# Attention and two FFN layers on one core: value products in a bank per tile, first queries loaded from ScalarE's queue, the second score pair moved behind the layer's first block, and a spare PSUM bank for one more block

## Chip, cores and metric

The kernel runs on one core of one Trainium2 chip. The metric is device time in microseconds of one execution; every time before the change is from three timed runs and one profiled execution.

## What is computed

```
scores = (q @ k.T) / 8; causal mask; a = softmax(scores); local = a @ v      # B=2, H=8, S=576, D=64
q_p = phi(q); mem = (q_p @ M_prev) / (q_p . z_prev + 1e-6)                   # phi = elu + 1
x = sigmoid(beta) * mem + (1 - sigmoid(beta)) * local                        # laid out as 1152 tokens x 512
x = relu(x @ w_in)^2 @ w_out                                                 # first layer, 512 -> 2048 -> 512, weights wider than fp32
out = sum_e p[:, e] * (relu(x @ w1[e]) @ w2[e])                              # four experts, 512 -> 1024 -> 512
```

## The kernel before

The 1152 tokens are nine tiles of 128, in three chunks: chunk 0 is tiles 7 and 8 (the first 128 positions of both batches), chunk 1 is tiles 0 to 3, chunk 2 is tiles 4 to 6. Attention of a chunk runs beside the first layer of the chunk before it, so the program has an **opening** (attention of chunk 0, and the first scores of chunk 1), a **first stage** (layer of chunk 0, with the rest of chunk 1's attention, about 20 to 133 us), a **second stage** (layer of chunk 1 with chunk 2's attention), then the layer of chunk 2 and the experts.

Attention works on pairs: the same heads of two tiles. `s_` makes the score matmuls of a pair into two PSUM buffers (tag `s`, of which the first stage has two), the row maxima by VectorE (`top`, L189), then the exponentials by ScalarE (L319). `t_` transposes on TensorE (`atp`), and a copy brings it to SBUF (`at`); `v_` multiplies by the values (`pv`). `phis` makes phi(q), `mem` multiplies it by the memory (`pm`).

In the opening a string of steps sets the order on every engine. Chunk 0's four units are (tile 7, heads 0-3), (8, 0-3), (7, 4-7), (8, 4-7). Before, a bank `pv` held four heads of both tiles, and `local(0)` (step `x0`) read both banks before `v1` and `v3` wrote tile 8's half of them. `c0.load(0)` issues the first keys and queries, and `beta` (tile `bt`) is loaded ahead of it on ScalarE's queue; the gate made from `bt` (L172, then L174 to L176 on VectorE) stands ahead of the first row maxima on VectorE.

The first layer works in 16 blocks f of 128 hidden columns: `up(f)` (four matmuls for chunk 0, `hpa`), squared ReLU (`g`), and two blocks later `down(f-2)` (four matmuls, `y`). Its weights come as 64-bit words (`w`, 512 KB a half block), which ScalarE (`mag`, `bits`, L694 and L697) and VectorE (L700, L703) turn into fp32; the result is used and also written to DRAM (`w1s`), from where chunk 1's and chunk 2's layers read it back (`wraw`).

`mix(main, side, ratio, due)` puts `ratio` steps of attention behind each step of the layer. On TensorE the program's order holds; on the other engines outside the opening a list scheduler decides, and SyncE issues nearly all DMAs in the order that it gives. DMAs take eight semaphores in turn (DMAHW0 to DMAHW7), so each issue waits until the eighth DMA before it has landed. In `up`, a block's sums go to the bank `h`, of which there is one, or for a block named `spare` to a buffer of the tag `s`.

Of the kernel before, what the change touches and what calls it, by code (L numbers as in the profile page):

```python
# [21 lines left out]
P = 128  # L22
B, H, S, D = 2, 8, 576, 64
# [14 lines left out]
CHUNKS = [(7, 9), (0, 4), (4, 7)]  # L38
# [14 lines left out]
def attention_then_experts(ctx, tc, qa, ka, va, qc, kc, vc, mz, beta, w1, probs, w2, out):  # L53
# [11 lines left out]
    nc = tc.nc  # L65
# [99 lines left out]
    bt = kv.tile([P, H], F32, name="bt")  # L165
# [61 lines left out]
    ka_t, va_t = {}, {}  # L227
# [29 lines left out]
    def attention_a(c, pool, eng, banks):  # L257
# [9 lines left out]
        def load(r):  # L267
            raw = pool.tile([P, H, P], F32, tag="qa", name="qa", bufs=2)
            ka_t[r] = kva.tile([P, H, P], F32, name=f"ka{r}")
            for hs in (slice(0, 4), slice(4, 8)):  # L270
                nc.sync.dma_start(out=ka_t[r][:, hs], in_=ka[r, :, hs])
                nc.sync.dma_start(out=raw[:, hs], in_=qa[r, :, hs])
            q[r] = [raw, None, pool.tile([P, B, H, D + 1], F32, tag="xm", name="xm", bufs=2)]
            if r:
                load_v(r)
# [63 lines left out]
        def v_(u):  # L339
            t, kn, h0, nh = u  # L340
            b = TILES[t][0][0]
            at = at_.pop(u)
            half = t - b, h0 // 4
            if b == 0 and h0 % 4 == 0:
                pvs[half] = banks[0].tile([P, B, H // 2, D], F32, tag="pv", name="pv", bufs=banks[3])
            pv = pvs[half]
            for i in range(nh):
                for k in range(kn // P):
                    j = i * kn + k * P
                    for p in range(0, P, 64):  # L350
                        nc.tensor.matmul(
                            pv[p:p + 64, b, h0 % 4 + i, :], lhsT=at[:, j + p:j + p + 64], rhs=va_t[b, k][:, h0 + i, :],
                            start=(k == 0), stop=(k == kn // P - 1),
                        )
            if c and b and (h0 + nh) % 4 == 0:
                if half[1] == 0:
                    xls[t - b] = pool.tile([P, B, H, D], F32, tag="xl", name="xl", bufs=2)
                nc.scalar.activation(out=xls[t - b][:, :, h0 + nh - 4:h0 + nh], in_=pv, func=AF.Copy)
# [46 lines left out]

        def local(b):
            xl = xls[b] = pool.tile([P, H, D], F32, tag="xl0", name="xl0", bufs=2)
            for i in range(2):
                hs = slice(4 * i, 4 * i + 4)
                nc.vector.tensor_mul(xl[:, hs], pvs[CHUNKS[0][0], i][:, b], fs[0][:, b, hs, None].to_broadcast([P, 4, D]))  # L410
            nc.vector.tensor_add(xl, xl, q[0][2][:, b, :, 0:D])

        def out_(b):
# [296 lines left out]
    def ffn1(c, ps, gp, nh, cv=None):  # L710
        t0, t1 = CHUNKS[c]
        n = (t1 - t0) * P
        per = 512 // n
        gs, ws = {}, {}

        todo = [x for g in range(n1 + 1) for x in ((g, 0), (g - 2, 1)) if 0 <= x[0] < n1] + [(n1 - 1, 1)]
        raws = {}

        def fetch(ahead):
            while c and todo and len(raws) < ahead:  # L720
                x = todo.pop(0)
                raws[x] = wrp.tile([P, DM], F32, tag="wraw", name="wraw")
                nc.sync.dma_start(out=raws[x], in_=w1s[x])

        def prep(f, half):
            if c == 0:
                while (f, half) not in made:
                    next(cv)
                ws[f, half] = made.pop((f, half))
                next(cv, None)  # L730
                return
            fetch(1)
            raw = raws.pop((f, half))
            w = wp.tile([P, 2, DM], F32R, tag=f"w{half}", name=f"w{half}")
            on_vector = ((f < 3, f % 4 == 3), (False, f % 2))[c - 1][half]
            split(w, raw, nc.vector if on_vector else nc.gpsimd)
            ws[f, half] = w
            fetch(2)

        def up(f):  # L740
            spare = c == 1 and f == 1
            hp = (ps if spare or f % nh else ps_h).tile([P, n], F32, tag="s" if spare else "h", bufs=2 if spare else 1, name="hp" + "abc"[c])
            yield from mm_in(c, hp, ws.pop((f, 0)))
            r = gp.tile([P, n], F32, tag="r", name="r") if c else gp.tile([P, n], F32, tag="g", name="g0", bufs=3)
            nc.scalar.activation(out=r, in_=hp, func=AF.Relu)
            nc.vector.scalar_tensor_tensor(out=r, in0=hp, scalar=0.0, in1=r, op0=ALU.max, op1=ALU.mult)  # L746
            if c == 0:
                gs[f] = r
                return
            g = gp.tile([P, 2, n], F32R, tag="g", name="g", bufs=3)  # L750
            nc.scalar.activation(out=g[:, 0], in_=r, func=AF.Copy)  # L751
            nc.vector.tensor_sub(g[:, 1], r, g[:, 0].bitcast(F32))  # L752
            gs[f] = g

        def down(f):
            w, g = ws.pop((f, 1)), gs.pop(f)
            for d in range(NK):
                first, last = f == 0 and d % per == 0, f == n1 - 1 and d % per == per - 1
                if c == 0:
                    nc.tensor.matmul(yacc[d], lhsT=w[:, d * P:(d + 1) * P], rhs=g, start=first, stop=last)  # L760
                for i, (a, b) in enumerate(PASS if c else ()):
                    nc.tensor.matmul(  # L762
                        yacc[d], lhsT=w[:, a, d * P:(d + 1) * P], rhs=g[:, b],
                        start=(first and i == 0), stop=(last and i == 2),
                    )
                for k in range(d - per + 1, d + 1) if last else ():
                    nc.scalar.activation(out=y_of(c)[:, k], in_=yacc[k], func=AF.Copy)
                yield

        prep(0, 0)  # L770
        ps = (yield) or ps
        banks = [ps.tile([P, per, n], F32, tag=f"y{d}", name=f"y{d}") for d in range(NK // per)]
        yacc = [banks[d // per][:, d % per, :] for d in range(NK)]
        for f in range(n1 + 2):
            if f + 1 < n1:
                prep(f + 1, 0)
            if 1 <= f <= n1:
                prep(f - 1, 1)
            if f < n1:
                yield from up(f)  # L780
            if f >= 2:
                yield from down(f - 2)
        for k in range(NK):
            junk = gp.tile([P, n], F32, tag="r", name="junk")
            nc.scalar.activation(out=junk, in_=y_of(c)[:, k], func=AF.Square, accum_out=ysq[:, c, k:k + 1])

    with ExitStack() as ca:
        kva = ca.enter_context(tc.tile_pool(name="kva", bufs=1))
        aap = ca.enter_context(tc.tile_pool(name="aap", bufs=2))
        cvp = ca.enter_context(tc.tile_pool(name="cvp", bufs=2))  # L790
        cv = convert(cvp)
        mzd = kva.tile([P, H, B, D + 1], F32, name="mzd")
        with tc.tile_pool(name="ps_0", bufs=1, space=PSUM) as ps_0:
            with tc.manual_schedule():
                nc.scalar.dma_start(out=bt, in_=beta.partition_broadcast(P))

                wt = aap.tile([P, 512], BF16, name="wt")
                nc.vector.memset(wt, 0.0)
                warm = ps_h.tile([P, 512], F32, tag="h", name="warm")
                for _ in range(8):  # L800
                    nc.tensor.matmul(warm, lhsT=wt[:, 0:P], rhs=wt, start=True, stop=True)
                nc.gpsimd.memset(ones, 1.0)
                masks()
                layer = ffn1(0, None, gp, 2, cv)
                banks = [ps_0, 3, 2, 2]
                c0, c1 = attention_a(0, aap, nc.vector, banks), attention_a(1, aap, nc.gpsimd, banks)
                c0.load(0)
                for b in range(B):
                    bs = slice(D * b, D * b + D)
                    nc.gpsimd.memset(mzd[bs, :, 1 - b], 0.0)  # L810
                    nc.sync.dma_start(out=mzd[bs, :, b], in_=mz[bs, b])
                c0.load_v(0)
                opening(c0, c1, layer)
        nc.sync.dma_start(out=mzt, in_=mz[0:D])
        with tc.tile_pool(name="ps_1", bufs=1, space=PSUM) as ps_1:
            banks[:] = ps_1, 2, 1, 1
            layer.send(ps_1)
            mix(layer, rest(c1, value_scale(aap, banks)), 0.58)
    with ExitStack() as cb:
        bp = cb.enter_context(tc.tile_pool(name="bp", bufs=1))  # L820
        with tc.tile_pool(name="ps_2", bufs=1, space=PSUM) as ps_2:
# [346 lines left out]
```

## Time and profile before

| | |
|---|---|
| median of 3 runs | 727.13 us (726.19 to 728.55) |
| the profiled execution | 726.71 us, of which the span of its profile is 724.9 us |
| busy over the span | TensorE 679.4 us (94%), VectorE 548.1 us (76%), ScalarE 428.2 us (59%), GpSimd 239.3 us (33%) |
| chain that ended last | TensorE 51%, VectorE 19%, ScalarE 12%, DMA 7%, issue 6%, GpSimd 3% |

Busy time is the sum over an engine's instructions; the chain is followed back from the last instruction to whatever released it each time. TensorE is nearly full as a mean, but not in the opening and the first 40 us, where the DMA queues are.

### The profile page before, as it was taken

To read this page: it belongs to the slowest core of one execution; us is meant where nothing else is said; L and a number is where in the kernel's file an instruction comes from. 1 tells how busy PE (TensorE), PEld (TensorE's weight loads), DVE (VectorE), ACT (ScalarE), POOL (GpSimd) and SP (SyncE) were. 2 spreads that over 40 slices of the span, in tenths; PEclk is the share of its full clock that TensorE was granted. 3 is DMA by queue.
4 is the path that set the end of the run, shared out by engine and by line. 5 is a ranking of instruction groups with operands and counts; after the bars stand their busy time and mean duration, and the time that the engine had idled before them with its cause. 6 is when DMAs were issued, how large, how long until landed. Compare 5 with 4: busy or idle time off the path is not lost.

```text
span 724.9 us, 12553 instructions
## 1 busy us (share of the span) xinstructions
PE 679.4 (94%) x4604; PEld 482.5 (67%) x4604; DVE 548.1 (76%) x1058; ACT 428.2 (59%) x842; POOL 239.3 (33%) x247
## 2 busy tenths in 40 slices
PE   7799899988999999989899999999999999999997
PEld 4577677766777778989665655666655555555553
DVE  7888776499979853667788778998787785867763
ACT  5888894666665546877786667455544343535340
POOL 1011003245242365545524423544332323242400
PEclk9999999999999999999999999999999999999999
DMA  8987983468875554875321322333333131100002
GB/s 304 343 312 234 305 259 91 172 214 208 192 172 118 126 108 125 284 247 156 103 89 59 117 84 92 117 117 117 115 118 117 60 113 62 59 1 1 1 1 72
DMA packets 65422, 101.25 MB, mean 140 GB/s; under 512 B 32656, under 2 KB 34704, under 8 KB 65360
## 3 DMA queue, kind: packets, MB, share of 16 engines
q1 hardware_dynamic: 65216, 100.45, 45.2%
q8 instruction: 36, 0.59, 0.3%
q14 instruction: 26, 0.21, 0.1%
q10 hardware_dynamic: 144, 0.00, 0.0%
HBM read 82.87 MB, written 10.75 MB: 129 GB/s over the span
## 4 chain that ended last, share of the span: by engine, by line
PE 51%; DVE 19%; ACT 12%; DMA 7%; issue 6%; POOL 3%; SPq 0%; DVEq 0%; ACTq 0%; POOLq 0%
PE o L1056 19%; PE pe L964 16%; DMA raw<-in_w 4%; PE y L762 4%; PE hpb L106 3%; PE y L760 2%; PE pv L619 2%; ACT a L319 2%; DMA wraw<-w1s 2%; DVE wu L928 2%; DVE g L752 1%; DVE a L189 1%; DVE w L873 1%; PE sc L551 1%; DVE g L980 1%
## 5 line engine op out<-in xcount | busy, mean ns | idle before, releaser
L1056 PE MATMUL o<-w,g 128*128 128x512 f16 x864 | 218.3, 379 | 6.9 <-DVE g L980 3.6
L964 PE MATMUL pe<-xs,wu 128*128 128x256 f16 (+1 forms) x1344 | 196.3, 286 | 1.9 <-DVE h L985 1.9
L964 PEld LDWEIGHTS <-wu 128*128 128x128 f16 x1344 | 131.0, 98 | 69.9 <-issue 3.5
L1056 PEld LDWEIGHTS <-g 128*128 128x128 f16 x864 | 83.8, 98 | 77.2 <-DVE g L980 6.6
L84 POOL TENSOR_TENSOR w<-wraw,w 128x512 fp32r<-128x512 f32 x49 | 72.5, 1484 | 144.6 <-ACT w L83 144.2
L979 ACT ACTIVATE g<-h 128x512 f16<-128x512 f32 (+1 forms) x64 | 43.3, 677 | 105.7 <-DVE h L985 105.7
L762 PE MATMUL y<-g,w 128*128 128x512 f32 (+1 forms) x384 | 90.7, 372 | 1.7 <-ACT w L83 0.9
L994 POOL TENSOR_TENSOR u<-u,p 128x256 f32<-128x256 f32 (+1 forms) x32 | 32.4, 1012 | 131.9 <-ACT p L993 111.0
L762 PEld LDWEIGHTS y<-g,w 128*128 128x128 f32 x384 | 68.2, 189 | 9.9 <-ACT w L83 1.2
L980 DVE SCALAR_TENSOR_TENSOR g<-h,g 128x512 f16<-128x512 f32 (+1 forms) x64 | 50.5, 788 | 25.5 <-ACT g L979 25.2
L985 DVE SCALAR_TENSOR_TENSOR h<-pe,u 128x256 f32<-128x256 f32 (+1 forms) x96 | 42.9, 452 | 19.8 <-PE pe L964 15.7
L106 PE MATMUL hpb<-x,w 128*128 128x512 f32 x192 | 53.2, 414 | 4.7 <-DVE r L746 4.6
L931 POOL TENSOR_TENSOR ws<-raw 128x256 f32<-128x256 f32 x32 | 23.3, 728 | 102.0 <-issue 79.8
L928 DVE SCALAR_TENSOR_TENSOR wu<-ws,wpow,wu 128x512 f16<-128x512 f32 x64 | 50.9, 835 | 2.9 <-ACT wu L939 2.9
L873 DVE SCALAR_TENSOR_TENSOR w<-raw,wpow,w 128x512 f16<-128x512 f32 x64 | 48.1, 755 | 0.7 <-ACT w L872 0.6
L83 ACT ACTIVATE w<-wraw 128x512 fp32r<-128x512 f32 x64 | 39.6, 622 | 14.9 <-DMA wraw<-w1s 8.4
L869 ACT ACTIVATE junk<-raw 128x1024 bf16<-128x1024 f32 x32 | 33.6, 1050 | 20.6 <-DMA raw<-in_w 20.5
L106 PEld LDWEIGHTS hpb<-x,w 128*128 128x128 f32 x192 | 36.3, 196 | 13.7 <-DVE r L746 6.5
L872 ACT ACTIVATE w<-raw,wpow 128x512 f16<-128x512 f32 x64 | 44.6, 709 | 0.9 <-PE o L1056 0.9
L106 PE MATMUL hpc<-x,w 128*128 128x384 f32 x192 | 37.9, 341 | 4.0 <-POOL w L84 3.1
L189 DVE CUSTOM_DVE_ANT_0 a<-sc,mask 128x384 f32<-128x384 f32 (+4 forms) x80 | 35.7, 477 | 5.5 <-PE sc L551 5.1
L752 DVE TENSOR_TENSOR g<-r,g 128x512 fp32r<-128x512 f32 (+1 forms) x32 | 30.7, 961 | 10.4 <-ACT g L751 9.8
(169 smaller groups left out, 1164.4 us busy)
## 6 DMA issues: line engine op xcount, KB each, us to landing
raw<-in_w SPq DMA_DIRECT2D x64, 512.0 KB, 3.4
w<-in_w SPq DMA_DIRECT2D x32, 512.0 KB, 5.3
wraw<-w1s SPq DMA_DIRECT2D x64, 256.0 KB, 3.0
w1s<-bits SPq DMA_DIRECT2D x32, 256.0 KB, 3.2
kraw<-in_kc SPq DMA_DIRECT2D x8, 576.0 KB, 4.1
vraw<-in_vc SPq DMA_DIRECT2D x8, 320.0 KB, 4.1
qraw<-in_qc SPq DMA_DIRECT2D x4, 512.0 KB, 4.7
out<-acc SPq DMA_DIRECT2D x8, 256.0 KB, 2.1
```

Source lines behind the costliest of these rows:

```text
L84: eng.tensor_sub(w[:, 1], raw, w[:, 0].bitcast(F32))
L106: nc.tensor.matmul(acc, lhsT=w[:, a, kk * P:(kk + 1) * P], rhs=xs_r[c][:, b, kk, :], start=(i == 0), stop=(i == 3 * NK - 1),)
L189: nc.vector.tensor_tensor_reduce(out=dst, in0=sc, in1=msk, op0=ALU.add, op1=ALU.max, scale=1.0, scalar=-3.0e38, accum_out=m)
L762: nc.tensor.matmul(yacc[d], lhsT=w[:, a, d * P:(d + 1) * P], rhs=g[:, b], start=(first and i == 0), stop=(last and i == 2),)
L872: nc.scalar.activation(out=w0, in_=x, func=AF.Copy, scale=s)
L873: nc.vector.scalar_tensor_tensor(out=w1, in0=x, scalar=s, in1=w0, op0=ALU.mult, op1=ALU.subtract)
L928: nc.vector.scalar_tensor_tensor(out=w[:, 1, ks], in0=x, scalar=s1, in1=w[:, 0, ks], op0=ALU.mult, op1=ALU.subtract)
L964: nc.tensor.matmul(acc, lhsT=w[:, wa, k, kk * P:kk * P + P], rhs=x[:, xb, kk], start=(m == 0), stop=(m == 5))
L979: nc.scalar.activation(out=g[:, 0], in_=hm, func=AF.Relu)
L980: nc.vector.scalar_tensor_tensor(out=g[:, 1], in0=hm, scalar=0.0, in1=g[:, 0], op0=ALU.max, op1=ALU.subtract)
L985: nc.vector.scalar_tensor_tensor(out=out, in0=acc, scalar=HID, in1=x, op0=ALU.mult, op1=ALU.add)
L1056: nc.tensor.matmul(outs[t], lhsT=g[:, gb, r:r + P], rhs=w[:, wa], start=(p == 0 and m == 1 and k == 0), stop=(p == 3 and m == 0 and k == 2),)
```

## The change

Five edits. `v_` takes one `pv` bank per tile of chunk 0 instead of one per half of the heads, and `local` multiplies all eight heads of a tile in one instruction. The first block of queries is issued from ScalarE's queue, and creating the two attention objects and `c0.load(0)` now stand ahead of the load of `bt`. The first stage's `mix` begins with a debt of -1.4 steps. In chunk 1's layer, block 2 takes a buffer of the tag `s` as block 1 does.

```diff
@@ load
-                nc.sync.dma_start(out=raw[:, hs], in_=qa[r, :, hs])
+                (nc.sync if r else nc.scalar).dma_start(out=raw[:, hs], in_=qa[r, :, hs])
@@ v_
-            half = t - b, h0 // 4
-            if b == 0 and h0 % 4 == 0:
+            half = (t - b, h0 // 4) if c else t
+            if h0 == 0 if c == 0 else b == 0 and h0 % 4 == 0:
                 pvs[half] = banks[0].tile([P, B, H // 2, D], F32, tag="pv", name="pv", bufs=banks[3])
...
-                            pv[p:p + 64, b, h0 % 4 + i, :], lhsT=at[:, j + p:j + p + 64], rhs=va_t[b, k][:, h0 + i, :],
+                            pv[p:p + 64, b if c else h0 // 4, h0 % 4 + i, :], lhsT=at[:, j + p:j + p + 64], rhs=va_t[b, k][:, h0 + i, :],
@@ local
-            for i in range(2):
-                hs = slice(4 * i, 4 * i + 4)
-                nc.vector.tensor_mul(xl[:, hs], pvs[CHUNKS[0][0], i][:, b], fs[0][:, b, hs, None].to_broadcast([P, 4, D]))
+            pv = pvs[CHUNKS[0][0] + b].rearrange("p i h d -> p (i h) d")
+            nc.vector.tensor_mul(xl, pv, fs[0][:, b, :, None].to_broadcast([P, H, D]))
             nc.vector.tensor_add(xl, xl, q[0][2][:, b, :, 0:D])
@@ up
-            spare = c == 1 and f == 1
+            spare = c == 1 and f in (1, 2)
@@ the opening
-                nc.scalar.dma_start(out=bt, in_=beta.partition_broadcast(P))
-
+                banks = [ps_0, 3, 2, 2]
                 wt = aap.tile([P, 512], BF16, name="wt")
                 nc.vector.memset(wt, 0.0)
+                c0, c1 = attention_a(0, aap, nc.vector, banks), attention_a(1, aap, nc.gpsimd, banks)
+                c0.load(0)
+                nc.scalar.dma_start(out=bt, in_=beta.partition_broadcast(P))
...
-                banks = [ps_0, 3, 2, 2]
-                c0, c1 = attention_a(0, aap, nc.vector, banks), attention_a(1, aap, nc.gpsimd, banks)
-                c0.load(0)
@@ the first stage
-            mix(layer, rest(c1, value_scale(aap, banks)), 0.58)
+            mix(layer, rest(c1, value_scale(aap, banks)), 0.58, -1.4)
```

On TensorE the scores of chunk 1's second pair stood behind three `hpa` matmuls and those of the third pair two `hpa` later; now they stand behind six and one more. Up to the first `pm` of chunk 1, twelve `hpa` and no `y` stood ahead of it, now twelve `hpa` and two `y`; up to the fourth pair's scores fifteen `hpa` and four `y`, now sixteen and five. The schedulers of the other engines answer with other orders, up to the first stage's end; from the second stage on the orders are nearly the same on every engine.

SyncE's queue at the first write of converted weights, before (`w1s` is that write, `w_398` and `w_419` the fifth and sixth word load, and the brackets name the semaphores waited for):

```order
L280 DMA va_2_613<-in_va 128x512 [waits DMAHW1_49]
L706 DMA w1s<-bits 128x512 [waits DMAHW2_49,DVE_49]
L682 DMA w_398<-in_w 128x1024 [waits DMAHW3_49,Activation_49]
L430 DMA vstage<-in_vc 128x4x128 [waits DMAHW4_49]
L706 DMA w1s<-bits 128x512 [waits DMAHW5_49,DVE_49]
L682 DMA w_419<-in_w 128x1024 [waits DMAHW6_49,Activation_49]
```

The same place after the change (`w_396` and `w_417` are now the fifth and sixth word load):

```order
L280 DMA va_2_611<-in_va 128x512 [waits DMAHW0_49]
L280 DMA va_2_613<-in_va 128x512 [waits DMAHW1_49]
L429 DMA vstage<-in_vc 128x4x128 [waits DMAHW2_49]
L429 DMA vstage<-in_vc 128x4x128 [waits DMAHW3_49]
L705 DMA w1s<-bits 128x512 [waits DMAHW4_49,DVE_49]
L681 DMA w_396<-in_w 128x1024 [waits DMAHW5_49,Activation_49]
L722 DMA wraw<-w1s 128x512 [waits DMAHW6_49,DMAHW4_49]
L705 DMA w1s<-bits 128x512 [waits DMAHW7_49,DVE_49]
L681 DMA w_417<-in_w 128x1024 [waits DMAHW0_49,Activation_49]
```

A read back of the first converted weights, `wraw`, has moved up to where it must wait for the write two rows ahead of it to land, and the sixth word load stands behind it.

ScalarE in the same stretch, before (each L319 row of four is one pair's exponentials):

```order
L697 ACTIVATE bits<-w_333 128x512
L319 ACTIVATE a,sm<-a,nb 128x256 x4
L694 ACTIVATE mag<-w_398 128x512
L697 ACTIVATE bits<-w_398 128x512
L694 ACTIVATE mag<-w_419 128x512
L745 ACTIVATE g_517<-hpa 128x256
L336 ACTIVATE at<-atp 128x512
L319 ACTIVATE a,sm<-a,nb 128x256 x4
L181 ACTIVATE phia<-qa 128x512 x2
```

and after:

```order
L696 ACTIVATE bits<-w_331 128x512
L693 ACTIVATE mag<-w_396 128x512
L696 ACTIVATE bits<-w_396 128x512
L693 ACTIVATE mag<-w_417 128x512
L696 ACTIVATE bits<-w_417 128x512
L319 ACTIVATE a,sm<-a,nb 128x256 x4
L693 ACTIVATE mag<-w_434 128x512
L744 ACTIVATE g_501<-hpa 128x256
L696 ACTIVATE bits<-w_434 128x512
L319 ACTIVATE a,sm<-a,nb 128x256 x4
L181 ACTIVATE phia<-qa 128x512 x2
```

The second pair's exponentials, which stood behind the fourth conversion, now stand behind the sixth.

VectorE in the same stretch after the change (`a_456` and `a_458` are the row maxima of the second pair, `bits_447` the fifth conversion):

```order
L699 SCALAR_TENSOR_TENSOR bits_438<-mag_436,bits_438 128x512
L189 ISA a_456,mx_354<-sc_455,mask_88 128x256
L189 ISA mx_354 128x1
L702 SCALAR_TENSOR_TENSOR bits_438<-w64_331,bits_438 128x512
L699 SCALAR_TENSOR_TENSOR bits_447<-mag_445,bits_447 128x512
L189 ISA a_456,mx_354<-sc_455,mask_88 128x256
L189 ISA mx_354 128x1
L702 SCALAR_TENSOR_TENSOR bits_447<-w64_396,bits_447 128x512
L313 TENSOR_SCALAR nb_355<-mx_354 128x2
L189 ISA a_458,mx_359<-sc_457,mask_88 128x256
```

Three of the second pair's four maxima now stand behind the fifth conversion; before, all four stood ahead of the fourth.

## Rows read from the trace of the kernel before

**Rows 1.** Busy time in four stretches, us (instructions); then clock, DMA share, GB/s.

```profile
20.00:40.00 20.00, 14.67 (x89) 11.44 (x87) 16.98 (x52) 18.27 (x49) 0.00 (x0) 0.92 1.00 356
40.00:80.00 40.00, 34.34 (x311) 27.11 (x310) 31.31 (x77) 33.14 (x79) 5.58 (x4) 1.00 0.82 275
80.00:133.00 53.00, 51.62 (x457) 41.34 (x458) 34.18 (x88) 35.38 (x84) 6.51 (x5) 1.00 0.56 180
140.00:160.00 20.00, 16.56 (x67) 12.86 (x66) 19.74 (x21) 13.83 (x21) 12.85 (x8) 0.91 0.65 206
```

**Rows 2.** DMA issues: beta, second half of queries; count, size, us to landing.

```profile
bt<-in_beta ACTq DMA_DIRECT2D x1, 4.0 KB, 3.3
...
qa<-in_qa SPq DMA_DIRECT2D x1, 256.0 KB, 5.8
```

**Rows 3.** Opening in order of time: start, us, engine; idle before and its releaser.

```profile
0.74 0.40 ACTq L795 DMA_DIRECT2D bt<-in_beta  x1
1.20 0.44 SPq L272 DMA_DIRECT2D qa<-in_qa  x1
2.15 0.43 SPq L272 DMA_DIRECT2D qa<-in_qa  x1
6.62 0.17 DVE L174 TENSOR_SCALAR bt<-bt 128x8 f32<-128x8 f32 x1
7.14 0.28 DVE L189 CUSTOM_DVE_ANT_0 a<-sc,mask 128x128 f32<-128x128 f32 x1
```

**Rows 4.** The opening's end in order of time, TensorE and VectorE.

```profile
17.04 0.76 DVE L410 TENSOR_TENSOR xl<-pv,f 128x256 f32<-128x256 f32 x2
17.52 1.15 PE L351 MATMUL pv<-va,at 128*64 128x64 f32 x32 [1.68 <-DVE xl L410]
17.83 0.69 DVE L411 TENSOR_TENSOR xl<-xl,xm 128x512 f32<-128x512 f32 x1
21.52 1.56 PE L101 MATMUL hpa<-y,bits 128*128 128x256 f32 x6 [0.74 <-ACT y L416]
```

**Rows 5.** DMA landings: ka issued at 13.93, w1s at 21.27, w at 38.41.

```profile
ka<-in_ka SPq DMA_DIRECT2D x1, 256.0 KB, 8.8
...
w1s<-bits SPq DMA_DIRECT2D x1, 256.0 KB, 5.3
...
w<-in_w SPq DMA_DIRECT2D x1, 512.0 KB, 4.5
```

**Rows 6.** SyncE's queue in order of time: start, us, issue.

```profile
13.93 0.46 SPq L271 DMA_DIRECT2D ka<-in_ka  x1
24.78 0.39 SPq L682 DMA_DIRECT2D w<-in_w  x1
```

**Rows 7.** ScalarE in order of time: sixth conversion and third pair's exponentials.

```profile
30.73 0.67 ACT L694 ACTIVATE mag<-w 128x512 f32<-128x512 f32 x1 [0.57 <-DMA w<-in_w]
32.05 0.51 ACT L319 ACTIVATE a<-a,nb 128x256 f32<-128x256 f32 x1
34.01 1.14 ACT L181 ACTIVATE phia<-qa 128x512 f32<-128x512 f32 x2
```

**Rows 8.** TensorE's stalls in the first stage, in order of time.

```profile
26.94 1.13 PE L302 MATMUL sc<-ka,qa 64*128 64x128 f32 x14 [1.29 <-DVE mx L189]
35.88 0.95 PE L364 MATMUL pm<-mzd,phia 128*128 128x130 f32 x6 [2.14 <-DVE phia L184]
36.65 1.89 PE L760 MATMUL y<-g,bits 128*128 128x256 f32 x4
46.25 1.03 PE L760 MATMUL y<-g,bits 128*128 128x256 f32 x4
```

**Rows 9.** Second stage: TensorE's stall, and two rows behind it.

```profile
148.25 4.62 PE L106 MATMUL hpb<-x,w 128*128 128x512 f32 x12 [3.44 <-DVE r L746]
...
155.60 0.68 DVE L746 SCALAR_TENSOR_TENSOR r<-hpb,r 128x512 f32<-128x512 f32 x1
...
156.64 0.96 PE L106 MATMUL hpb<-x,w 128*128 128x512 f32 x3
```

## The prediction

> **What bounds the kernel now.** The busy shares on the page, in the table above, say TensorE; but four of the five edits lie in the first 133 us, so the shares of that part come first. In 20 to 40 us TensorE works 14.67 of 20 us, ScalarE 18.27, VectorE 16.98, and the DMA engines all of the time [rows 1]. There the first layer waits for its weights: word loads land, ScalarE and VectorE convert them, and TensorE waits behind both. From 40 to 80 us TensorE idles 40 - 34.34 = 5.7 us and ScalarE 6.9; from 80 to 133 us TensorE idles 1.4 of 53 [rows 1] and is the bound. So a shift made before 40 us counts only as far as it is still there at 80. The timeline names TensorE's stalls: 1.29 us for row maxima and 2.14 for phi(q), after which two `y` (four records) took 1.89 us where two at 46.25 took 1.03 [rows 8]; the mean granted clock of 20 to 40 us is 0.92 against 1.00 later [rows 1]. In the second stage one stall of 3.44 us stands ahead of a block's first matmul [rows 9].
>
> **First queries on ScalarE's queue, beta behind them.** Before, the first half of the queries is issued behind a key load, at 1.20 us, the second at 2.15, and beta at 0.74 [rows 3]. Now both queues start near 0.74, so the first half can be 1.20 - 0.74 = 0.46 us earlier, at most. The Trainium skill (DMA: Bandwidth & Descriptors, section "Issuing engines are not separate DMA queues") holds that DMAs of several engines run on the same 16 DMA engines, so that a second issuer saves its sequencer's time only, which speaks against more; that cap is the one the rows give. Against this stands beta, 4 KB, which is now third on its queue, at about 0.74 + 2 x 0.44 = 1.6 us. It landed 3.3 us after its issue [rows 2], which would give 4.9 and cost nothing; but behind a query half on the same queue it may land with that half, which took 5.8 us [rows 2], at 2.15 + 5.8 - 0.46 = 7.5. I take 7.5, from the row nearest in kind, a load behind another one on its queue. VectorE's gate instructions stand ahead of the first maxima: from 6.62 to 7.14 they take 0.5 [rows 3], and ScalarE's exponential about 0.2 ahead of them, so the maxima begin at 8.3, not 7.14: 1.2 us late (bounds -0.46 and +1.2), and what is queued behind them is all of the opening's VectorE work.
>
> **A bank per tile.** TensorE's wait of 1.68 us for VectorE's read of the shared bank goes [rows 4]. But VectorE did not wait for it: its `local` pair ran through, and the transposes that follow need VectorE's result. What is left is one 512-wide multiply (0.69, as the sum's instruction beside it) instead of two that take 17.83 - 17.04 = 0.79, per tile, 0.2 in all [rows 4], and chunk 1's scores ahead of the transposes, so that these follow each tile at once: 0.5 us. With the late start the first `hpa` moves from 21.52 [rows 4] to about 22.0.
>
> **The second pair behind the first block.** Here the order on the queues decides. SyncE now meets a read back of converted weights whose write stands two rows ahead. That write needs a semaphore that `ka`, issued at 13.93 [rows 6], holds until it lands 8.8 us later [rows 5], so it goes at 22.8; a write in this stretch took 5.3 us [rows 5]: 28.1. Only then go the read back, a write and the sixth word load, each some 0.4 us on the queue [rows 6]: 28.8, where it went at 24.78 [rows 6]. It lands 4.5 us later, as the load of 38.41 did with little in front of it [rows 5], at 33.3; at most 5.9, as the load of 24.78, for which ScalarE waited until 30.73 [rows 6, 7]. The fifth load, at about 23.4, lands near 29.2 by the same 5.9. ScalarE, in order, converts both before the second pair's exponentials, and VectorE has three of that pair's maxima behind the fifth conversion. So a wait takes the place of the 1.29 us at 26.94 [rows 8]: TensorE has the third pair's scores, which need the second pair's buffers, only near 33, and idles some 5 us ahead of them.
>
> From the sixth load on, ScalarE sets the pace: two conversion instructions (0.57 between starts, a little under the 0.67 that one shows [rows 7]) 1.1, four exponentials 34.01 - 32.05 = 2.0 [rows 7], three small ones 1.4, four exponentials 2.0, so phi begins at 33.3 + 6.5 = 39.8, not 34.01 [rows 7]. `pm` followed phi's start by 35.88 - 34.01 = 1.9 [rows 7, 8]: 41.7 instead of 35.88, **5.8 late**, with two `y` more done (1.0 [rows 8]). Behind `pm` the clock should be back, since TensorE works between the stalls: the 1.89 becomes 1.03, and the six further matmuls before the fourth pair's scores gain as much again, 1.7 in all; at those scores one `hpa` and one `y` more are done, as the orders show. That leaves 5.8 - 1.0 - 1.7 = **3.1 us** behind. The 1.2 us of beta are not added: they end before the fifth load lands.
>
> **What is given back by 80 us.** TensorE had 5.7 us idle in 40 to 80, ScalarE 6.9, and 1.7 in 20 to 40 [rows 1]. ScalarE's new idle, for the fifth load (about 1.6) and the sixth (33.3 - 30.4 = 2.9), less the 0.57 that went [rows 7], is 3.9 of these 8.6, so it can finish the same work by 80; and it has more conversions behind it by then, which are what TensorE's stalls there wait for in the end. I take the 3.1 as given back: 0 at 80 us, between +3.1 (nothing) and 3.1 - 5.7 = -2.6 (all of the idle).
>
> **Spare bank.** The 3.44 us are a wait for the square of block 2, since blocks 2 and 3 shared a bank [rows 9]. Now block 3 starts at once; but block 4 takes that bank next and needs the square of block 3, which VectorE does at 155.60 to 156.3, in the same order as before, and in 140 to 160 us VectorE is busy 19.74 of 20 [rows 1, 9]. Block 4 started at 156.64 [rows 9], so the stall moves there and at most 156.64 - 156.3 = 0.3 us is gained. Without that cover it would be 3.44 and the slow clock behind it (12 records in 4.62 us, where 3 at 156.64 took 0.96 [rows 9]: 0.8), 4.2 us.
>
> **Sum.** Against the profiled execution's 726.71: 0 from the first stage, -0.3 from the spare bank: 726.4. The median of three runs is 0.4 above that execution, so 726.8. A measurement of this kernel tells about 0.3%, 2.2 us, from no change, so this is no change: 724.9 to 729.3 around 727.13.
>
> **Rivals.**
>
> *Not given back* (slower). The idle of 40 to 80 us may not lie where the delay can use it: its stalls may wait for loads that are themselves issued later because of the read back. It decides at the fourth pair's scores: if `pm` is 5.8 late and TensorE keeps its idle of 5.7 us behind it [rows 1], the 3.1 stay: 727.13 + 3.1 - 0.3 = 729.9, and 731 with the load's longer landing (1.4). For it speaks that ScalarE is nearly full; against, that its balance of 8.6 us covers 3.9.
>
> *The stalls go* (faster). If the conversions done ahead free the rest of the stage, TensorE loses the idle of 40 to 80, -2.6 by the bound above, or more if the sixth load lands early enough that the stall at 27 us is small: then the 1.29, the 2.14 and the slow clock's 1.7 [rows 8] are gained as well, up to 5. I price it at 723.5. For it speaks that TensorE waits for conversions there; against, the queue order above.
>
> *The spare bank pays in full* (faster): -4.2, 722.9. It needs VectorE to square block 3 earlier, against a VectorE with 0.26 us idle in 20.
>
> *Nothing of the edits arrives* (no change): the DMA share of 1.00 in 20 to 40 us [rows 1] sets the pace, as the loads are the same bytes, and all before is hidden: 726.4 to 727.1, beside my forecast and not told from it.
>
> **Numbers.** Forecast 0.36 and nothing arrives 0.10, both no change; not given back 0.22, all slower; the stalls go 0.26 and the spare bank in full 0.06, faster. So faster 0.32, same 0.46, slower 0.22. The forecast's own range is 724.9 to 729.3. From the faster rivals to the slower one, with the bounds of the landing, the range is 722.5 to 730.5; it leaves out about 1 in 10 on each side.
>
> **What the new profile would show.** The first maxima on VectorE near 8.3 us (near 6.7 if beta does not wait). No wait of `pv` for `xl`. ScalarE waiting for a word load at `mag` twice, ending near 29 and 33; TensorE idle for about 5 us ahead of the third pair's scores; `pm` of chunk 1 near 41.7. At 80 us both traces at the same point of the layer. In the second stage no stall ahead of block 3 and one ahead of block 4. The prediction is wrong if the sixth load lands before 31, if TensorE's idle in 40 to 80 us stays near 5.7, or if block 3's square moves up.

## The result and the profile after

The changed kernel takes 731.42 us (median of 11 runs, 729.62 to 735.5) where the kernel before took 727.13 (724.62 to 729.27, 11 runs): a ratio of 1.0066, 95% interval 1.0048 to 1.0084. It is slower by 4.3 us between the medians, 4.8 by the ratio, and lies above the predicted range.

The profiled execution is the slowest of the 11: 735.5 us, with a span of 733.7. So first, where its excess over the kernel before arises, by the timeline of TensorE. The kernel before:

```profile
43.39 1.16 PE L302 MATMUL sc<-ka,qa 64*128 64x128 f32 x16
...
79.84 0.94 PE L364 MATMUL pm<-mzd,phia 128*128 128x130 f32 x6 [1.59 <-DVE x L223]
...
133.56 8.54 PE L106 MATMUL hpb<-x,w 128*128 128x512 f32 x36
...
416.80 0.39 PE L1056 MATMUL o<-w,g 128*128 128x512 f16 x1 [1.03 <-ACT g L979]
```

The same places after:

```profile
46.98 1.16 PE L302 MATMUL sc<-ka,qa 64*128 64x128 f32 x16
...
84.63 0.94 PE L364 MATMUL pm<-mzd,phia 128*128 128x130 f32 x6 [1.47 <-DVE x L223]
...
136.84 8.54 PE L106 MATMUL hpb<-x,w 128*128 128x512 f32 x36
...
425.13 0.39 PE L1054 MATMUL o<-w,g 128*128 128x512 f16 x1 [3.12 <-ACT g L977]
```

The fourth pair's scores are 3.6 us late, the `pm` near 80 us 4.8, the second stage's first matmul 3.3. The last row is of another kind: the experts are the same code, and a stall of 3.12 stands where 1.03 stood. Of the 8.8 us between the two spans about half lies behind 300 us, and I take that half for this execution's own, since the medians differ by 4.3 and the profile of after_one_spare below, with the same experts, has a stall of 1.17 there.

The opening, which was to be 0.5 us late (ScalarE, VectorE, TensorE; answers to [rows 3, 4]):

```profile
4.87 0.63 ACT L181 ACTIVATE phia<-qa 128x512 f32<-128x512 f32 x1 [1.44 <-DMA qa<-in_qa]
6.58 0.21 ACT L172 ACTIVATE bt<-bt 128x8 f32<-128x8 f32 x1 [1.08 <-DMA bt<-in_beta]
6.70 0.61 ACT L181 ACTIVATE phia<-qa 128x512 f32<-128x512 f32 x1
7.35 0.28 DVE L189 CUSTOM_DVE_ANT_0 a<-sc,mask 128x128 f32<-128x128 f32 x1
...
15.90 1.44 PE L351 MATMUL pv<-va,at 128*64 128x64 f32 x32
...
17.27 1.16 PE L302 MATMUL sc<-ka,qa 64*128 64x128 f32 x16
```

Beta is there at 6.58, between the bounds of 4.9 and 7.5, and the first maxima start 0.2 us late (7.35 for 7.14). The wait of 1.68 ahead of `pv` is gone and chunk 1's scores start 1.3 us earlier (17.27 for 18.60); the first `hpa` stands at 21.39 (21.52 before).

SyncE's queue, then ScalarE's conversions and phi, then TensorE (answers to [rows 6 to 8]):

```profile
21.93 0.44 SPq L705 DMA_DIRECT2D w1s<-bits  x1
22.53 0.34 SPq L681 DMA_DIRECT2D w<-in_w  x1
27.45 0.33 SPq L722 DMA_DIRECT2D wraw<-w1s  x1
27.86 0.38 SPq L705 DMA_DIRECT2D w1s<-bits  x1
28.34 0.38 SPq L681 DMA_DIRECT2D w<-in_w  x1
```

```profile
32.62 0.66 ACT L693 ACTIVATE mag<-w 128x512 f32<-128x512 f32 x1 [2.71 <-DMA w<-in_w]
...
39.29 1.13 ACT L181 ACTIVATE phia<-qa 128x512 f32<-128x512 f32 x2
```

```profile
31.08 0.76 PE L302 MATMUL sc<-ka,qa 64*128 64x128 f32 x2 [3.78 <-issue]
32.48 2.04 PE L302 MATMUL sc<-ka,qa 64*128 64x128 f32 x14 [0.64 <-DVE mx L189]
34.46 3.59 PE L101 MATMUL hpa<-y,bits 128*128 128x256 f32 x8
...
41.14 0.94 PE L364 MATMUL pm<-mzd,phia 128*128 128x130 f32 x6 [0.93 <-DVE phia L184]
```

SyncE issues nothing from 22.9 to 27.45, until the first write has landed; the sixth word load goes at 28.34 (24.78 before), its conversion starts at 32.62, phi at 39.29, `pm` at 41.14. The windows, which answer to [rows 1]:

```profile
20.00:40.00 20.00, 13.69 (x72) 10.54 (x72) 14.58 (x47) 14.67 (x41) 0.00 (x0) 0.83 0.99 342
40.00:80.00 40.00, 34.73 (x316) 27.65 (x315) 33.70 (x80) 33.34 (x76) 5.58 (x4) 1.00 0.81 266
80.00:133.00 53.00, 50.69 (x452) 39.64 (x450) 31.95 (x90) 38.47 (x93) 6.09 (x5) 1.00 0.56 188
```

ScalarE's idle in 20 to 40 us grew from 1.7 to 5.3 us, and the mean granted clock of these 20 us fell from 0.92 to 0.83. From 40 to 80 TensorE still idles 5.3 us, where it idled 5.7: the room that was to take the delay up was not used.

### The profile page after: what moved, and what is told of

Read it like the earlier page. It is cut to its first block, busy times and chain, and to the rows that moved or that the text cites. A ratio compares the mean times of both kernels' runs of the same rounds, so it can differ in the third digit from the quotient of the medians.

```text
span 733.7 us, 12557 instructions
## 1 busy us (share of the span) xinstructions
PE 686.9 (94%) x4604; PEld 488.5 (67%) x4604; DVE 546.7 (75%) x1056; ACT 429.3 (59%) x842; POOL 238.9 (33%) x247
## 4 chain that ended last, share of the span: by engine, by line
PE 56%; DVE 15%; ACT 11%; DMA 9%; issue 5%; POOL 3%; SPq 0%; DVEq 0%; ACTq 0%; POOLq 0%
PE o L1054 19%; PE pe L962 16%; PE y L761 5%; DMA raw<-in_w 4%; PE hpb L106 3%; PE hpc L106 3%; PE y L759 2%; PE pv L618 2%; PE sc L550 2%; ACT a L319 2%; DMA wraw<-w1s 2%; DMA w<-in_w 1%; POOL w L84 1%; DVE g L978 1%; DVE bits L699 1%
## 5 line engine op out<-in xcount | busy, mean ns | idle before, releaser
L84 POOL TENSOR_TENSOR w<-wraw,w 128x512 fp32r<-128x512 f32 x49 | 72.4, 1484 | 142.7 <-ACT w L83 142.2
L761 PE MATMUL y<-g,w 128*128 128x512 f32 (+1 forms) x384 | 92.7, 378 | 1.3 <-POOL w L84 0.7
L761 PEld LDWEIGHTS y<-g,w 128*128 128x128 f32 x384 | 69.7, 193 | 9.7 <-POOL w L84 0.9
L83 ACT ACTIVATE w<-wraw 128x512 fp32r<-128x512 f32 x64 | 39.6, 623 | 12.1 <-PE y L761 6.6
```

The source lines that it names most:

```text
L83: nc.scalar.activation(out=w[:, 0], in_=raw, func=AF.Copy)
L84: eng.tensor_sub(w[:, 1], raw, w[:, 0].bitcast(F32))
L761: nc.tensor.matmul(yacc[d], lhsT=w[:, a, d * P:(d + 1) * P], rhs=g[:, b], start=(first and i == 0), stop=(last and i == 2),)
```

## The experiments

Theory A: the delay comes from SyncE's queue, which waits with the read back, and the queries' move to ScalarE's queue put the read back there: the program's order with that edit undone has none ahead of the sixth load. Rival B: it comes from the order that the debt of -1.4 gives ScalarE, the second pair's exponentials behind the sixth conversion. C: the second spare bank costs, by the slow clock behind a stall that moved. The first four runs tell these apart.

**after_sync_queue**, the queue edit undone in the kernel after:

```diff
-                (nc.sync if r else nc.scalar).dma_start(out=raw[:, hs], in_=qa[r, :, hs])
+                nc.sync.dma_start(out=raw[:, hs], in_=qa[r, :, hs])
```

> The kernel after with one edit undone: the first queries are again issued on SyncE's queue. Without that edit the program's order on SyncE has the sixth word load directly behind the second write of converted weights, with no read back in between (the two vstage loads are again spread out too). Theory A, the read back on SyncE's queue is what the loss of 4.3 us comes from, and the queue edit is what brought it there: third pair's scores near 28.7 us instead of 31.08, and the median within 1.5 us of the kernel before, 726 to 728.5. Theory B, the loss comes from the moved second pair, whose exponentials stand behind the sixth conversion: the order on ScalarE is unchanged here, so the median stays at 730 to 732. Theory C, the spare bank costs 1.0 us (a wait of 4.77 us at block 4 and the slow clock behind it): 1.0 above what A says, 727.5 to 729.

**order_only**, the kernel before with the debt alone:

```diff
-            mix(layer, rest(c1, value_scale(aap, banks)), 0.58)
+            mix(layer, rest(c1, value_scale(aap, banks)), 0.58, -1.4)
```

> The kernel before with one edit: the first stage's mix begins with -1.4. The second pair's exponentials stand behind the sixth conversion on ScalarE, but no read back stands on SyncE's queue ahead of the sixth load. Theory A (read back): 726 to 728.5, and the sixth conversion starts at 30 to 31 us as before (30.73). Theory B (order on ScalarE): 729.5 to 731.5, first stage's end 3 us later than before. Theory C says nothing of this run.

**opening_only**, the kernel after without the debt and with one spare block:

```diff
-            mix(layer, rest(c1, value_scale(aap, banks)), 0.58, -1.4)
+            mix(layer, rest(c1, value_scale(aap, banks)), 0.58)
...
-            spare = c == 1 and f in (1, 2)
+            spare = c == 1 and f == 1
```

> The kernel after without the -1.4 and without the second spare block: the queue edit and the bank per tile alone. The read back stands ahead of the sixth word load. Theory A (read back): 729.5 to 731.5, with the sixth load landing at 32 to 33 us. Theory B (order on ScalarE): 726.5 to 727.5, since the second pair's exponentials stand ahead of the fifth conversion as before.

**spare_only**, the kernel before with the second spare block (the last two lines of that diff, the other way round).

> The kernel before with one edit: block 2 of chunk 1's layer also takes a spare bank. The prediction's step: the stall moves from block 3 to block 4, a gain of 0.3 us, median 726.8. Theory C: the stall at block 4 comes with matmuls at the slow clock behind it that nothing covers any more (in the kernel after 1.65, 1.05 and 2.52 us where 0.96, 0.63 and 1.55 stood), so a loss of 0.7 to 1.7 us, 727.8 to 728.8.

All kernels together, the later ones too. The last two columns are starts in the timeline of TensorE of one profiled execution each, less those of the kernel before (43.39 and 133.56).

| kernel | median, us | median of before beside it | ratio (95%) | fourth pair's scores | second stage |
|---|---|---|---|---|---|
| after | 731.42 | 727.13 | 1.0066 (1.0048 to 1.0084) | +3.6 | +3.3 |
| after_sync_queue | 729.41 | 726.51 | 1.0036 (1.0014 to 1.0059) | +2.8 | +3.2 |
| order_only | 727.88 | 726.51 | 1.0019 (1.0000 to 1.0039) | +2.1 | +2.2 |
| opening_only | 731.06 | 726.51 | 1.0062 (1.0044 to 1.0080) | +4.6 | +7.8 |
| spare_only | 727.60 | 726.51 | 1.0023 (1.0010 to 1.0037) | -0.3 | -0.1 |
| opening_reads_gpsimd | 731.29 | 727.28 | 1.0060 (1.0045 to 1.0076) | +2.2 | +4.0 |
| after_reads_gpsimd | 729.70 | 727.28 | 1.0032 (1.0017 to 1.0047) | +2.3 | +2.6 |
| bank_only | 728.98 | 727.28 | 1.0019 (1.0000 to 1.0038) | -0.4 | +2.8 |
| after_one_spare | 731.27 | 727.28 | 1.0052 (1.0032 to 1.0071) | +5.0 | +4.6 |
| queue_only | 730.51 | 726.95 | 1.0046 (1.0026 to 1.0066) | +2.8 | +5.4 |
| queue_reads_gpsimd | 728.85 | 726.95 | 1.0017 (1.0000 to 1.0035) | -0.9 | +1.7 |
| extra_load | 726.44 | 726.95 | 0.9986 (0.9967 to 1.0004) | -0.9 | +0.6 |
| extra_read | 729.32 | 726.95 | 1.0032 (1.0014 to 1.0050) | +4.2 | +4.1 |

The debt alone costs about 1.4 us by the medians (its interval reaches to nothing), the opening's edits without it 4.5, nearly all of the loss: B cannot be the whole. But the third pair's scores in order_only, from its timeline of TensorE:

```profile
30.96 0.77 PE L302 MATMUL sc<-ka,qa 64*128 64x128 f32 x2 [3.48 <-issue]
```

With no read back ahead of the sixth load TensorE idles there as long as after the change. So that stall is the debt's (the second pair's maxima and exponentials stand behind the conversions), and the value of 28.7 that A gave for after_sync_queue was wrong too: it measured 31.05 there. Undoing the queue edit took 2.0 us off the medians and left 2.9; its 729.41 lies in none of the three ranges, above those of A and C and below that of B. C holds by the median of spare_only (+1.1, just under its range); the place is below.

The next four runs ask whether the read back or the queue edit itself costs (rival Q), and what the bank per tile does, and what the second spare block costs behind a late first stage.

**opening_reads_gpsimd** and **after_reads_gpsimd**, the kernels opening_only and after with the first three read backs on GpSimd's queue:

```diff
-                nc.sync.dma_start(out=raws[x], in_=w1s[x])
+                (nc.gpsimd if c == 1 and x in ((0, 0), (1, 0), (2, 0)) else nc.sync).dma_start(out=raws[x], in_=w1s[x])
```

> The kernel of opening_only (queue edit and bank per tile) with the first three read backs issued from GpSimd's queue, which has nothing else to do there; SyncE's queue then has the sixth word load directly behind the second write. The orders of TensorE, ScalarE and VectorE stay as in opening_only up to about 50 us, and the queue edit itself stays. Theory A (the blocked queue): the sixth load goes at 24 to 25 us, its conversion starts at 30 to 31 instead of 34.16, and the median falls from 731.06 to 726.5 to 728. Rival Q (the queue edit costs by itself, by beta behind the queries or by the loads that crowd the opening): the median stays at 730 to 731.5 and the sixth conversion near 34.

> The kernel after with the first three read backs issued from GpSimd's queue, all five edits kept. Theory A: the read back is worth what undoing the queue edit was worth, so the median is near that of after_sync_queue, 728.5 to 730. If the queue edit has a cost besides the read back: 730.5 to 732. What is left over the kernel before should be the order (about 1.4 us) and the spare bank (about 1.1 to 1.7).

**bank_only**, opening_only with the queries back on SyncE's queue (the diff of after_sync_queue).

> The kernel after with the queue edit, the -1.4 and the second spare block undone: the bank per tile alone, with beta's load behind the first keys and queries. The prediction's step: 0.2 and 0.5 us earlier at the opening's end, of which nothing need arrive, 726 to 727. From the sums of the runs so far (after_sync_queue less order_only and spare_only): -0.6 to +0.4, 726 to 727.

**after_one_spare**, the kernel after with one spare block.

> The kernel after with the second spare block undone, the other edits kept. If the spare bank costs the same behind a late first stage as in spare_only (1.1 to 1.7 us): 729.5 to 730.5, with a stall of about 3.4 us at block 3 and none over 1 at block 4. If it costs nothing there, as the prediction's step of -0.3 has it: 731 to 732.

after_reads_gpsimd lands where undoing the queue edit had landed (1.0032 and 1.0036): in the changed kernel the read back is worth some 2.5 us (1.0066 less 1.0032), though from 35 us on ScalarE's order differs there too. In opening_reads_gpsimd the delay at the fourth pair halves (+4.6 to +2.2), but the median stays (731.29), against A; its profiled execution, 729.63, is the fastest of its six. bank_only was to cost nothing and costs 1.7, at the edge of its interval: it is ahead at the fourth pair and 2.8 late by the second stage. after_one_spare, at 731.27, lies where a spare block that costs nothing had been put, and 0.2 us under the changed kernel by the medians. Moving TensorE's scores ahead of the transposes had also changed the orders of ScalarE and VectorE. So theory O: every new order of the two converting engines costs by itself, and the read back may be innocent. The last four runs hold the orders fixed.

**queue_only**, the kernel before with the queries on ScalarE's queue and `bt` behind them; on TensorE, ScalarE and VectorE every instruction of the first stage stands where it stood:

```diff
-                nc.scalar.dma_start(out=bt, in_=beta.partition_broadcast(P))
...
-                nc.sync.dma_start(out=raw[:, hs], in_=qa[r, :, hs])
+                (nc.sync if r else nc.scalar).dma_start(out=raw[:, hs], in_=qa[r, :, hs])
...
                 c0.load(0)
+                nc.scalar.dma_start(out=bt, in_=beta.partition_broadcast(P))
```

> The kernel before with the queue edit alone: the first queries on ScalarE's queue and beta's load behind them. The orders of TensorE, ScalarE and VectorE are those of the kernel before, instruction for instruction, through the first stage; on SyncE the read backs stand ahead of the sixth, the seventh and the tenth word load. Theory A (the blocked queue): sixth conversion at 33 to 34.5 us instead of 30.73, fourth pair's scores 2 to 4 us late, median 729.5 to 731.5. Theory O (what costs is that the edits changed the orders of ScalarE and VectorE, and the read back is hidden): 726 to 728.

**queue_reads_gpsimd**, the same with the first three read backs on GpSimd's queue.

> queue_only with the first three read backs on GpSimd's queue; the orders of TensorE, ScalarE and VectorE are again those of the kernel before. Theory A: the sixth word load goes at 24 to 25 us and the median is that of the kernel before or, by an opening that starts its second scores 0.7 us earlier, up to 0.5 under it: 726 to 727.5. Rival Q (the queue edit costs by its own loads): 728.5 or more, with the first hpa later than 22.5.

**extra_load** and **extra_read**, the kernel before with one more 256 KB transfer on SyncE's queue, a load or a read back of the first write; nobody reads what it brings:

```diff
             nc.sync.dma_start(out=w1s[f, half], in_=bits.bitcast(F32))
+            if i == 0:
+                extra = pool.tile([P, DM], F32, tag="extra", name="extra", bufs=1)
+                nc.sync.dma_start(out=extra, in_=va[0, 0])      # extra_load
+                nc.sync.dma_start(out=extra, in_=w1s[f, half])  # extra_read
```

> The kernel before with one more 256 KB load (of values, into a buffer that nobody reads) on SyncE's queue behind the first write of converted weights, which waits for no write: it costs a place on the queue and bytes, where the read back also waits. Orders of ScalarE and VectorE as before. Theory A: the wait is what costs, so this costs the bytes only, at most 1 us: 726.5 to 728. Rival B2 (the bytes cost, as the DMA engines are busy all of 20 to 40 us): 256 KB at 356 GB/s are 0.7 us for each load behind, 728 or more.

> The same with the extra load reading back the first converted weights, so that SyncE's queue waits for the first write to land (about 26.5 us) ahead of the fifth word load, which went at 22.45 us. Fifth and sixth load go 4 and 3 us later than before. Theory A with the prediction's give back: the delay is gone by 80 us, 726.5 to 727.5. Theory A with the delay carried (TensorE's idle of 40 to 80 us starts from its own scores and moves with it): 729.5 to 732.

SyncE's queue and the sixth conversion in queue_only:

```profile
23.43 0.34 SPq L682 DMA_DIRECT2D w<-in_w  x1
28.36 0.33 SPq L723 DMA_DIRECT2D wraw<-w1s  x1
28.77 0.39 SPq L706 DMA_DIRECT2D w1s<-bits  x1
29.25 0.38 SPq L682 DMA_DIRECT2D w<-in_w  x1
...
33.96 0.66 ACT L694 ACTIVATE mag<-w 128x512 f32<-128x512 f32 x1 [2.69 <-DMA w<-in_w]
```

and in queue_reads_gpsimd, with GpSimd's queue:

```profile
25.81 0.38 SPq L682 DMA_DIRECT2D w<-in_w  x1
...
31.11 0.69 ACT L694 ACTIVATE mag<-w 128x512 f32<-128x512 f32 x1
...
28.26 0.71 POOL L723 DMA_DIRECT2D wraw<-w1s  x1 [24.02 <-DMA w1s<-bits]
```

With the same orders on the computing engines the queue edit costs 3.6 us and, with the read back waiting on a queue where no word load stands behind it, 1.9, an interval that reaches to zero. In the two timelines the wait is worth 3.7 us at the fourth pair and 3.7 at the second stage, between the medians 1.7. So A's mechanism holds, and O does not explain the 3.6; but A's range for queue_reads_gpsimd (726 to 727.5) was missed, and Q's two signs came: 728.85, and a first `hpa` at 22.56. The second sign does not tell, for extra_load, whose opening is that of the kernel before, has its first `hpa` at 22.59. In both the granted clock of 8 to 20 us is 0.86, where the kernel before has 1.00. What is left of the queue edit (Q) is between 0 and 2.5 us and stays open.

extra_load costs nothing measurable, so neither a place on the queue nor 256 KB more are the price. Up to the fourth pair extra_read differs from it in the wait, in two `vstage` loads (0.94 us on the queue) that also stand ahead of the fifth word load, and in two neighbouring ScalarE instructions exchanged:

```profile
22.41 0.94 SPq L430 DMA_DIRECT2D vstage<-in_vc  x2
26.70 0.34 SPq L709 DMA_DIRECT2D extra<-w1s  x1
27.14 0.54 SPq L682 DMA_DIRECT2D w<-in_w  x1
...
32.26 0.66 ACT L694 ACTIVATE mag<-w 128x512 f32<-128x512 f32 x1 [3.47 <-DMA w<-in_w]
...
35.48 1.12 PE L331 MATMUL atp<-ident,a 128*128 128x128 f32 x4 [4.37 <-ACT at L336]
...
47.64 1.16 PE L302 MATMUL sc<-ka,qa 64*128 64x128 f32 x16
...
83.40 0.94 PE L364 MATMUL pm<-mzd,phia 128*128 128x130 f32 x6 [1.66 <-DVE x L223]
...
137.68 2.66 PE L106 MATMUL hpb<-x,w 128*128 128x512 f32 x10
```

The fifth load goes 4.7 us later than before; from 23.35 to 26.70 SyncE only waits for the write. The delay is 4.2 us at the fourth pair, 3.6 at 80 us and 4.1 at the second stage: up to there it is carried, not given back. The median is 2.4 up (2.9 over extra_load); where the rest goes is below.

## Why the prediction was wrong

**The step that failed** is "What is given back by 80 us": "I take the 3.1 as given back: 0 at 80 us". The delay itself was sized well: sixth load at 28.34 (predicted 28.8), `pm` at 41.14 (41.7). The 3.1 counts work: at the fourth pair's scores two more matmuls of the layer are done than before, so that they start 3.6 us late but are some 2.6 behind in work, an estimate from the 1.03 us of two [rows 8]. At the `pm` near 80 us three more are done: 4.8 late, some 3.3 behind in work. At the second stage the work is the same again, and the delay 3.3. Nothing of it was given back. That is the rival "Not given back", 729.9 to 731, and its condition came true: TensorE kept its idle of 40 to 80 us. One term of the delay was right in size but not in place: behind `pm` the slow matmuls are gone as predicted (four `y` records in 1.03 us at 41.92), but they now stand ahead of it, where eight `hpa` records take 3.59 us (34.46 above) and eight at 21.39 took 1.97.

Why the idle could not be used is read from the rows, not tested by itself. ScalarE and VectorE before the change, around the fifth pair's scores (TensorE, at 51.53) and up to TensorE's next transposes at 55.05, which wait 1.52 us for the maxima:

```profile
46.63 0.49 ACT L319 ACTIVATE a<-a,nb 128x256 f32<-128x256 f32 x1
...
50.39 0.70 ACT L697 ACTIVATE bits<-w 128x512 int32<-128x512 uint8 x1
...
52.50 1.41 DVE L703 SCALAR_TENSOR_TENSOR bits<-w,bits 128x512 int32<-128x512 int32 x1
53.84 0.68 DVE L700 SCALAR_TENSOR_TENSOR bits<-mag,bits 128x512 int32<-128x512 int32 x1
54.44 0.55 DVE L189 CUSTOM_DVE_ANT_0 a<-sc,mask 128x384 f32<-128x384 f32 x1
```

and after it, TensorE's scores at 55.76 and next transposes at 58.90, with a wait of 1.14:

```profile
49.34 0.66 ACT L693 ACTIVATE mag<-w 128x512 f32<-128x512 f32 x1 [2.04 <-DMA w<-in_w]
...
50.47 0.50 ACT L319 ACTIVATE a<-a,nb 128x256 f32<-128x256 f32 x1
...
54.49 0.69 ACT L696 ACTIVATE bits<-w 128x512 int32<-128x512 uint8 x1
...
56.35 1.42 DVE L702 SCALAR_TENSOR_TENSOR bits<-w,bits 128x512 int32<-128x512 int32 x1
57.69 0.68 DVE L699 SCALAR_TENSOR_TENSOR bits<-mag,bits 128x512 int32<-128x512 int32 x1
58.29 0.55 DVE L189 CUSTOM_DVE_ANT_0 a<-sc,mask 128x384 f32<-128x384 f32 x1
```

The fifth pair's maxima wait for the conversions ahead of them on VectorE; these wait for ScalarE's `bits`, which stand on ScalarE behind the fourth pair's exponentials, and those need the fourth pair's scores. So the row starts with a result of TensorE's own, and all of it is 3.6 to 4.2 us late. From the fourth pair's scores to the `pm` near 80 us TensorE's stalls in the timeline sum to 5.65 us before (six, of 0.19 to 1.59) and 6.23 after (seven, of 0.41 to 1.50). The idle that I counted as room was the time of these passes from engine to engine, which each pass needs again.

The rival named another cause, loads that are themselves issued later. They add to the delay but are not needed to carry it: from 40 to 85 us ScalarE waits for word loads 4.0 us in queue_only, 2.0 after the change and not at all before, and the delay in queue_only grows from 2.8 at the fourth pair to 5.1 at the `pm` near 80 us; in extra_read it waits 0.2, and the delay stays (4.2, then 3.6).

Further on there is idle of the other kind. From 300 to 356 us TensorE waits for weights read back, which ScalarE and GpSimd prepare (`w`, L83 and L84): 4.96 us in seven stalls before, 2.79 in four in extra_read, whose delay falls there from 4.1 to 2.4. These stalls end with the preparation of weights and not with a result of attention that TensorE made just before, and there part of the delay was given back. In the profiled execution after the change this does not show: its granted clock of 310 to 330 us is 0.83, where the kernel before has 1.00.

**The queue edit** was priced at -0.46 to +1.2 us and its real price was put under another edit. I wrote the read back into the part on the second pair; it came with the queries' move, which takes two DMAs off SyncE's queue, and stands there in queue_only and opening_only without the debt. By the Trainium skill (DMA: Bandwidth & Descriptors, section "Issuing engines are not separate DMA queues") a second issuer saves only the time on its sequencer. The first query half agrees: it was used no earlier (4.87 after, 4.88 before). The second, issued at 1.18 instead of 2.15, does so only roughly: in queue_reads_gpsimd TensorE had it at 6.02, in the runs that load it from SyncE's queue at 6.7 to 8.3, so it came 0.7 to 2.3 us earlier where its issue is 0.97 earlier.

**The debt** alone costs 1.4 us (0 to 2.8 by the ratio). The wait ahead of the third pair's scores comes as the steps said, from the order on ScalarE and VectorE (31.08, predicted near 33); that the cost comes from this wait is read from the rows, not tested.

**The bank per tile** gave what was promised in the opening (no wait; in bank_only the first `hpa` at 21.03, 0.5 us earlier, of 0.7 promised). Not foreseen was that it changes the orders behind: alone it costs 1.7 us between the medians (0 to 2.8 by the ratio). In its profile two stalls of `tp` and `pm` near 80 us, 1.25 and 1.26, stand for one of 1.59; but 1.0 of its 2.8 us is there at the sixth pair's scores already (60.91 for 59.92), behind a stall of 1.93 for 1.52 and a granted clock of 0.85 around it, for 1.00. That the new orders cause all this is not shown.

**The spare bank.** The stall moved to block 4, as forecast:

```profile
159.61 1.65 PE L106 MATMUL hpb<-x,w 128*128 128x512 f32 x3 [4.77 <-DVE r L745]
161.06 1.05 PE L550 MATMUL sc<-kst,qh 128*128 128x512 f32 x2
161.91 2.52 PE L106 MATMUL hpb<-x,w 128*128 128x512 f32 x6
```

Block 4 is 3.0 late where the stage began 3.3 late: the 0.3 us of gain are there. But three matmuls take 1.65 where they took 0.96 [rows 9], with more slow ones behind: TensorE had idled 4.77 us, and as I read the rows the full VectorE no longer covers the slow clock behind the stall, as it did when the stall stood one block earlier. spare_only has the same rows without the other edits:

```profile
156.25 1.65 PE L106 MATMUL hpb<-x,w 128*128 128x512 f32 x3 [4.78 <-DVE r L746]
```

Its block 4 starts 0.4 us early, and 20 us on TensorE is 0.4 late (the `hpb` at 176.92 for 176.50): 0.8 us are lost behind the stall and 0.5 since the stage's start, where the prediction had a gain of 0.3. The median of spare_only, +1.1 us (by the ratio 0.7 to 2.7), agrees with such a cost; its profiled execution (726.49) is no slower than that of the kernel before (726.71), since it is ahead again behind 300 us. after_one_spare does not settle it: 1.0 us under after by the ratios, whose intervals overlap.

The four prices alone sum to 0.0107, or 7.8 us; together they cost 4.8. Debt and read back delay the same matmul, the fourth pair's scores, by 2.1 (order_only) and 2.8 (queue_only), and all edits together by 3.6; so the prices overlap. No combination that was run is faster than the kernel before.

Open: why the median of opening_reads_gpsimd did not fall as the delay at its fourth pair did, and what the queue edit costs without the read back.

## What to carry to other kernels

Before idle time is counted as room for a delay, ask what ends each piece of it: a stall that begins with the waiting engine's own result moves along with the delay and gives nothing back; one that ends with other work can shrink, as those behind 300 us did. An issue queue is a resource with an order: a transfer that waits for a write on its own queue holds every load behind it, and taking two unrelated transfers off the queue can bring it there. Where a scheduler decides, hold its orders fixed in the experiments; only so did the 3.6 us of the queue edit stand apart from those of new orders.

## What was not expected of the hardware

One more 256 KB load, in a stretch where the DMA engines were busy all of the time by the windows, cost nothing measurable (0.9986, 0.9967 to 1.0004). A 4 KB load behind two of 256 KB on its queue was there at 6.58 us, 4.9 after its issue at 1.67; ahead on the queue it had landed 3.3 us after its issue [rows 2].

The opening comes in two kinds. In the fourteen profiles the first `hpa` starts at 21.0 to 21.7 us where the granted clock of 8 to 20 us is 1.00, and at 22.2 to 22.7 where it is 0.72 to 0.86: five of the seven with the queue edit, and extra_load, which leaves the opening as it was. About 1 us of a start in the first stage can come from that alone.
